# Decoding float64 weights by bits alone, in a three-layer kernel on one core

## The chip, the cores and the metric

One core of a Trainium2 chip runs the whole program. The metric is device time in microseconds (us) for one execution, from the first to the last instruction; the time of a kernel is the median of its runs. The engines are named as in the profile: PE is TensorE (PEld its weight loads), DVE is VectorE, ACT is ScalarE, POOL is GpSimd, SP is SyncE. The suffix q marks an engine's queue.

## The reference

Three layers follow one another on 4 sequences of 576 positions with 512 features.

1. Attention with 8 heads of 64, half of them masked to the last 32 positions (local), half to positions of the same residue modulo 32 (strided).
2. A mixture of 4 causal attention experts of which each position takes 2: projections wq, wk, wv, a gate, softmax, and wo.
3. A convolutional feed-forward layer:

```python
h = np.maximum(x @ w_in, 0.0)                      # w_in: 512 x 1024
conv_out = sum(conv_w[k] * hp[:, k:k + S, :] for k in range(3))   # hp: h padded by one position
gate = 1.0 / (1.0 + np.exp(-conv_out))
out = (h * gate @ w_out).astype(np.float32)        # w_out: 1024 x 512
```

The three weights of the last layer, w_in, conv_w and w_out, reach the chip as float64. Each value is two 32-bit words, the low word first; the high word holds the sign, the 11 bits of the exponent and the first 20 bits of the mantissa, the low word the other 32 bits.

## The kernel before, in words

The work is cut into generators, one for each tile or unit, and a hand-written list of letters says in which order the generators are started. S is the first layer (16 units: batch by local or strided by half of the heads), J loads and splits the projections of the second layer, P computes its projections, A its attention units, W prepares w_in and conv_w, O prepares w_out, M is a step of the third layer. A step of one generator ends at a `yield`, and all live generators are advanced in turn. The program is built with a model of the instructions' times that puts each engine's instructions in order, so work without a dependency can be placed ahead of its letter.

Products in higher precision are made from a high and a low part of each operand. For w_out, `split64` decodes a tile of 128 x 256 values and writes the high part (wout[0], rounded by an ACT copy) and the low part (wout[1]). For w_in, `w_wp` decodes 128 x 512 values into one float32 tile wi, and PE multiplies it with wo's transpose (tile wps, line 774): 2 halves of 4 tiles, so 8 tiles numbered 0 to 7 here. `w_taps` decodes conv_w into taps, 128 x 24.

The decode of one tile (`f64_parts`) has these steps:

- L719, ACT: the absolute value of the high word, into c (tile fc for w_in, oc for w_out, taps for conv_w);
- L720, DVE: c is held between two limits;
- L721, DVE: c shifted left by 3 and masked to 30 bits;
- L723, DVE: sign and top exponent bit of the high word ored with c, written over the high word. This is a float32 number a, cut after 20 bits of mantissa;
- L725, DVE: the mask keeps only the sign and exponent of a, into c;
- line 726, an ACT copy (it shows as L99): the low word is converted from integer to float and scaled;
- L727, POOL: the product of that and c, f.

Then L735 or L769 (on POOL and DVE in turn) or L789 (POOL) adds f: for w_in and the taps a + f is the value; for w_out the high part is copied from a, `sub` (L108) takes a minus the high part into c, and L735 adds f to that.

The staging tiles of w_in and conv_w (st, five buffers, shared with J) are filled by SP's queue; wi and fc have two buffers each. The tiles of w_out (ow, two buffers, shared with the output tile ob) are filled by POOL's queue, and oc shares two buffers with a tile of the third layer. The space of the staging pool is handed to wout once w_in and the taps are done (`rel`).

Of the kernel before, what the change touches and what calls it, by code (L numbers as in the profile page):

```python
# [7 lines left out]
F32 = mybir.dt.float32  # L8
# [5 lines left out]
ALU = mybir.AluOpType  # L14
# [34 lines left out]
def moe_stack_kernel(ctx, tc, qk_in, vloc, vstr, w_p, wo_t, w_in, conv_w, w_out, out):  # L49
# [27 lines left out]
    act, dve, gp = nc.scalar, nc.vector, nc.gpsimd  # L77
# [3 lines left out]
    def eng(kind, b=0):  # L81
        n = turn[kind] = turn.get(kind, -1) + 1
        s = ENG[kind].split("|")[0 if b < EARLY else -1]
        return s[n % len(s)]

    def e2(kind, b=0):
        return dve if eng(kind, b) == "V" else gp
# [10 lines left out]
    def copy_a(out, in_, scale=1.0):  # L98
        act.activation(out=out, in_=in_, func=ACTF.Copy, scale=scale)  # L99
# [7 lines left out]
    def sub(eng, out, a, b):  # L107
        eng.tensor_tensor(out=out, in0=a, in1=b, op=ALU.subtract)  # L108
# [77 lines left out]
    taps = wts.tile([128, 3 * KF], F32, name="taps")  # L186
# [523 lines left out]
    stg = tc.alloc_tile_pool(name="stg", bufs=2)  # L710
    woT = stg.tile([128, KD, E * D], F32, tag="woT", bufs=1, name="woT")

    def f64_parts(words, c):


        wl, wh = words[:, :, 0], words[:, :, 1]
        f = wl.bitcast(F32)
        cu = c.bitcast(U32)
        act.activation(out=c, in_=wh.bitcast(F32), func=ACTF.Abs)  # L719
        e2("w1").tensor_scalar(out=c, in0=c, scalar1=F64_LO, scalar2=F64_HI, op0=ALU.max, op1=ALU.min)  # L720
        dve.tensor_scalar(out=cu, in0=cu, scalar1=3, scalar2=0x3FFFFFFF,  # L721
                          op0=ALU.logical_shift_left, op1=ALU.bitwise_and)
        dve.scalar_tensor_tensor(out=wh, in0=wh, scalar=0xC0000000, in1=cu,  # L723
                                 op0=ALU.bitwise_and, op1=ALU.bitwise_or)
        dve.tensor_scalar(out=cu, in0=wh, scalar1=0xFF800000, scalar2=None, op0=ALU.bitwise_and)  # L725
        copy_a(f, wl, 2.0 ** -52)
        e2("wf").tensor_tensor(out=f, in0=f, in1=c, op=ALU.mult)  # L727
        return wh.bitcast(F32), f

    def split64(words, c, hi, lo):  # L730
        a, f = f64_parts(words, c)
        copy_a(hi, a)
        yield
        sub(e2("wc"), c, a, hi.bitcast(F32))
        e2("wa").tensor_tensor(out=lo, in0=c, in1=f, op=ALU.add)  # L735
        yield

    def w_proj(kk):
# [20 lines left out]
    def w_wp(hf, kk):  # L759
        cs = slice(512 * hf, 512 * hf + 512)  # L760
        t = stg.tile([128, 512, 2], U32, tag="st", bufs=ST_BUFS, name="st")
        nc.sync.dma_start(out=t.rearrange("p n w -> p (n w)"), in_=w_in[128 * kk:128 * kk + 128, cs].bitcast(U32))
        for _ in range(8):
            yield
        wi = stg.tile([128, 512], F32, tag="wi", name="wi")
        fc = stg.tile([128, 512], F32, tag="fc", name="fc")
        yield
        a, f = f64_parts(t, fc)
        e2("wa").tensor_tensor(out=wi, in0=a, in1=f, op=ALU.add)  # L769
        yield  # L770
        if kk == 0:
            wps[hf] = [ps_o.tile([128, 512], F32, tag=f"o{r}", name="wps") for r in range(2)]
        for r in range(2):
            nc.tensor.matmul(out=wps[hf][r], lhsT=woT[:, kk, 128 * r:128 * r + 128], rhs=wi,
                             start=kk == 0, stop=kk == KD - 1)
        if kk == KD - 1:
            yield
            for r in range(2):
                copy_a(wp[0][:, r, cs], wps[hf][r])
                sub(dve, wp[1][:, r, cs], wps[hf][r], wp[0][:, r, cs].bitcast(F32))  # L780
            if hf == 1:
                done.add("wp")

    def w_taps():
        t = stg.tile([128, 1024], U32, tag="st", bufs=ST_BUFS, name="ct")[:, 0:2 * 3 * KF].rearrange("p (n w) -> p n w", w=2)
        nc.sync.dma_start(out=t.rearrange("p n w -> p (n w)"), in_=conv_w.bitcast(U32))
        yield
        a, f = f64_parts(t, taps)
        gp.tensor_tensor(out=taps, in0=a, in1=f, op=ALU.add)  # L789
        yield  # L790
        done.add("taps")

    def w_out_part(f, hf):
        cs = slice(256 * hf, 256 * hf + 256)
        t = late["g"].tile([128, 256, 2], U32, tag="ob", bufs=2, name="ow")
        c = late["h"].tile([128, 256], F32, tag="t", name="oc")
        nc.gpsimd.dma_start(out=t.rearrange("p n w -> p (n w)"), in_=w_out[128 * f:128 * f + 128, cs].bitcast(U32))
        yield
        yield from split64(t, c, wout[0][:, f, cs], wout[1][:, f, cs])
        done.add(("wout", f, hf))  # L800
# [27 lines left out]
    def rel():  # L828
# [9 lines left out]
        "J": [w_proj(kk) for kk in range(KD)],  # L838
        "P": [u for b in range(B) for u in p_items(b)],
        "W": [w_init(), w_wo()] + [w_wp(hf, kk) for hf in range(2) for kk in range(KD)] + [w_taps()],  # L840
        "A": [u for b in range(B) for u in a_items(b)],
        "O": [w_out_part(f, hf) for f in range(KF) for hf in range(2)],
# [74 lines left out]
```

## Time and profile before

| | before |
|---|---|
| median of 3 runs | 471.08 us (469.86 to 472.1) |
| span of the profiled execution | 471.1 us |
| PE busy | 407.7 us (87%) |
| DVE busy | 349.1 us (74%) |
| ACT busy | 313.0 us (66%) |
| POOL busy | 187.6 us (40%) |
| mean granted TensorE clock | 0.946 of full speed |

The profiled execution's time is its span. Busy time is the sum of an engine's instructions; an engine that is busy for a small share of the whole may be full in one stage. "Idle before" is the time that an engine sat idle just ahead of an instruction, and the arrow names what ended it. A line can be that of a helper: L99 is `copy_a`, L108 is `sub`, so groups of such lines are told apart by their tiles.

### The profile page before, as it was taken

The numbers are of one execution on the slowest core, as the hardware profiler recorded it, in microseconds if no ns is written. First come the engines' busy times: TensorE is split into PE (matmuls) and PEld (weight loads), VectorE is DVE, ScalarE is ACT, GpSimd is POOL, SyncE is SP. The second block draws the span as 40 slices with busy tenths as digits, with TensorE's granted clock in tenths as the row PEclk, the third lists the DMA queues.
The fourth block names the chain that finished last, engine by engine and source line by source line (L and its number), as shares of the span: only waits on it lengthen the run. The fifth ranks groups of instructions, "written<-read, shape, count | busy, mean of one in ns | idle before, by whom it ended". The sixth has DMA issues, their size and how long they took to land.

```text
span 471.1 us, 12502 instructions
## 1 busy us (share of the span) xinstructions
PE 407.7 (87%) x4736; PEld 295.2 (63%) x4736; DVE 349.1 (74%) x941; ACT 313.0 (66%) x836; POOL 187.6 (40%) x253
## 2 busy tenths in 40 slices
PE   3367789966999898879999999998999989999994
PEld 2253456653567666647776767776777557787872
DVE  7399996777589998999777677669578676565550
ACT  3164642658777848777776688778499785667662
POOL 4356873443246565546533123214122324223231
PEclk9997898997689989978999999999999899999998
DMA  6995842433866664394333415424324273101011
GB/s 193 304 321 161 208 116 58 120 98 98 127 147 147 142 120 132 87 153 63 97 58 89 84 31 79 96 46 68 58 63 97 55 119 85 45 1 45 0 47 45
DMA packets 104956, 48.30 MB, mean 103 GB/s; under 512 B 77504, under 2 KB 100032, under 8 KB 104896
## 3 DMA queue, kind: packets, MB, share of 16 engines
q1 hardware_dynamic: 103616, 43.31, 41.3%
q0 software_dynamic: 1280, 4.20, 3.1%
q8 instruction: 37, 0.61, 0.6%
q14 instruction: 23, 0.19, 0.2%
HBM read 27.56 MB, written 4.72 MB: 69 GB/s over the span
## 4 chain that ended last, share of the span: by engine, by line
PE 47%; DVE 25%; DMA 10%; ACT 8%; issue 7%; SPq 1%; POOL 0%; POOLq 0%; ACTq 0%; DVEq 0%
PE o L111 6%; PE o L112 6%; PE o L113 5%; DMA apt<-pn 5%; PE zav L579 4%; PE hps L111 4%; PE asc L529 4%; DMA un<-in_dram 3%; PE hps L112 3%; PE hps L113 3%; DVE t L640 2%; DMA ow<-in_dram 2%; PE psq L111 2%; DVE apf L533 2%; PE psq L113 2%
## 5 line engine op out<-in xcount | busy, mean ns | idle before, releaser
L640 DVE SCALAR_TENSOR_TENSOR t<-hs,taps,t 128x256 f32<-128x256 f32 x144 | 80.7, 567 | 34.6 <-ACT t L99 33.4
L108 POOL TENSOR_TENSOR pn<-apf,pn 64x64 f16<-64x64 f32 (+4 forms) x40 | 33.9, 848 | 81.4 <-ACT pn L99 66.1
L108 POOL TENSOR_TENSOR gl<-t,gh 128x512 fp32r<-128x512 f32 x36 | 47.2, 1312 | 47.6 <-ACT gh L99 23.7
L112 PE MATMUL o<-wout,gl 128*128 128x512 f32 x144 | 59.0, 409 | 1.4 <-POOL gl L108 1.4
L111 PE MATMUL o<-wout,gh 128*128 128x512 f32 x144 | 54.8, 418 | 3.3 <-ACT gh L99 3.1
L113 PE MATMUL o<-wout,gh 128*128 128x512 f32 x144 | 56.5, 392 | 0.0
L539 ACT ACTIVATE apf<-apf,anm 64x64 f32<-64x64 f32 (+4 forms) x80 | 44.3, 554 | 10.6 <-DVE anm L533 10.5
L579 PE MATMUL zav<-apt,v 128*64 128x128 f16 (+2 forms) x720 | 37.1, 231 | 8.9 <-DMA apt<-pn 5.8
L533 DVE CUSTOM_DVE_ANT_0 apf<-asc,m_c 64x64 f32<-64x64 f32 (+4 forms) x80 | 32.5, 421 | 15.7 <-PE asc L529 15.2
L111 PE MATMUL psq<-xt,wqk 128*128 128x288 f16 x128 | 37.9, 296 | 6.9 <-DVE qk L478 4.2
L111 PE MATMUL hps<-z,wp 128*128 128x258 f32 x128 | 41.9, 327 | 0.5 <-ACT hs L103 0.5
L579 PEld LDWEIGHTS <-v 128*64 128x64 f16 (+1 forms) x720 | 25.4, 113 | 25.2 <-issue 12.6
L103 ACT ACTIVATE hs<-hps 128x257 f32<-128x257 f32 (+2 forms) x72 | 27.5, 381 | 20.2 <-PE hps L113 19.8
L99 ACT ACTIVATE t<-hs,taps 128x256 f32<-128x256 f32 x72 | 36.0, 505 | 3.8 <-DVE wout L735 1.1
L112 PE MATMUL psq<-xt,wqk 128*128 128x288 f16 x128 | 37.5, 293 | 0.0
L113 PE MATMUL psq<-xt,wqk 128*128 128x288 f16 x128 | 37.4, 292 | 0.0
L112 PE MATMUL hps<-z,wp 128*128 128x258 f32 x128 | 37.0, 289 | 0.0
L113 PE MATMUL hps<-z,wp 128*128 128x258 f32 x128 | 36.9, 288 | 0.0
L112 PEld LDWEIGHTS o<-wout,gl 128*128 128x128 f32 x144 | 27.0, 188 | 10.0 <-POOL gl L108 3.1
L111 PEld LDWEIGHTS o<-wout,gh 128*128 128x128 f32 x144 | 24.8, 190 | 11.8 <-ACT gh L99 5.7
L529 PE MATMUL asc<-qk,qk 64*128 64x288 f16 (+4 forms) x192 | 31.4, 288 | 0.0
L562 DVE SCALAR_TENSOR_TENSOR pn<-apf,aden,pn 64x64 f16<-64x64 f32 (+4 forms) x40 | 24.1, 604 | 9.5 <-ACT pn L99 9.3
(166 smaller groups left out, 1072.0 us busy)
## 6 DMA issues: line engine op xcount, KB each, us to landing
ow<-in_dram POOLq DMA_DIRECT2D x16, 256.0 KB, 3.9
st<-in_dram SPq DMA_DIRECT2D x8, 512.0 KB
out_dram<-ob SPq DMA_DIRECT2D x16, 256.0 KB
un<-in_dram SPq DMA_DIRECT2D x16, 252.0 KB
vs<-in_dram SPq DMA_DIRECT2D x32, 72.0 KB
vn<-in_dram SPq DMA_DIRECT2D x16, 128.0 KB
un<-in_dram SPq DMA_DIRECT2D x8, 240.0 KB
st<-in_dram SPq DMA_DIRECT2D x4, 386.0 KB
```

What stands on the lines that cost most here:

```text
L99: act.activation(out=out, in_=in_, func=ACTF.Copy, scale=scale)
L103: act.activation(out=out, in_=in_, func=ACTF.Relu)
L108: eng.tensor_tensor(out=out, in0=a, in1=b, op=ALU.subtract)
L111: nc.tensor.matmul(out=out, lhsT=ah, rhs=bh, start=first, stop=False)
L112: nc.tensor.matmul(out=out, lhsT=al, rhs=bh, start=False, stop=False)
L113: nc.tensor.matmul(out=out, lhsT=ah, rhs=bl, start=False, stop=last)
L529: nc.tensor.matmul(out=scs[par], lhsT=qk[a][p0:p0 + 64, 0, q0:q0 + rows], rhs=qk[l][p0:p0 + 64, 1, c0:c0 + cw], start=n == 0, stop=n == 2)
L533: dve.tensor_tensor_reduce(out=pfs[par][:, c0:c0 + cw], in0=scs[par], in1=m_c[:rows, S - w + c0 if rows == 128 else S - 128:][:, :cw], sca ...
L539: act.activation(out=pfs[par], in_=pfs[par], func=ACTF.Exp, scale=-1.0, bias=nm[:, par, len(cuts) - 1:len(cuts)], accum_out=den[:, par:par ...
L562: dve.scalar_tensor_tensor(out=pn[:, 1, :w], in0=pfs[par], scalar=den[:, par:par + 1], in1=pn[:, 0, :w], op0=ALU.mult, op1=ALU.subtract)
L579: nc.tensor.matmul(out=av[64 * par:64 * par + 64, 0:rows], lhsT=v2[a][:kk, kb, D * e:D * e + D], rhs=pts[par][:kk, l, kb], start=(kb == 0 ...
L640: dve.scalar_tensor_tensor(out=tv, in0=taps_at[i][n], scalar=w, in1=tv, op0=ALU.mult, op1=ALU.add)
```

## The change

The low word is no longer converted to a number. Its top three bits are shifted down by 29 and ored behind the 20 bits of mantissa from the high word, which gives all 23 bits of a float32. The function `f64_word` writes that value into c; mask, conversion, product and sum are gone. In `split64` the high part is copied from c, and `sub` writes c minus the high part straight into the low part. In `w_wp` the tile fc is gone, and wi is the tile that all steps of the decode write. The number of `yield` steps stays. The lower 29 bits of the low word are not used.

```diff
-    def f64_parts(words, c):
+    def f64_word(words, c):
         wl, wh = words[:, :, 0], words[:, :, 1]
-        f = wl.bitcast(F32)
         cu = c.bitcast(U32)
         act.activation(out=c, in_=wh.bitcast(F32), func=ACTF.Abs)
         e2("w1").tensor_scalar(out=c, in0=c, scalar1=F64_LO, scalar2=F64_HI, op0=ALU.max, op1=ALU.min)
         dve.tensor_scalar(out=cu, in0=cu, scalar1=3, scalar2=0x3FFFFFFF,
                           op0=ALU.logical_shift_left, op1=ALU.bitwise_and)
-        dve.scalar_tensor_tensor(out=wh, in0=wh, scalar=0xC0000000, in1=cu,
+        dve.scalar_tensor_tensor(out=cu, in0=wh, scalar=0xC0000000, in1=cu,
                                  op0=ALU.bitwise_and, op1=ALU.bitwise_or)
-        dve.tensor_scalar(out=cu, in0=wh, scalar1=0xFF800000, scalar2=None, op0=ALU.bitwise_and)
-        copy_a(f, wl, 2.0 ** -52)
-        e2("wf").tensor_tensor(out=f, in0=f, in1=c, op=ALU.mult)
-        return wh.bitcast(F32), f
+        dve.scalar_tensor_tensor(out=cu, in0=wl, scalar=29, in1=cu,
+                                 op0=ALU.logical_shift_right, op1=ALU.bitwise_or)

     def split64(words, c, hi, lo):
-        a, f = f64_parts(words, c)
-        copy_a(hi, a)
-        yield
-        sub(e2("wc"), c, a, hi.bitcast(F32))
-        e2("wa").tensor_tensor(out=lo, in0=c, in1=f, op=ALU.add)
+        f64_word(words, c)
+        copy_a(hi, c)
+        yield
+        sub(e2("wc"), lo, c, hi.bitcast(F32))
         yield
...
         wi = stg.tile([128, 512], F32, tag="wi", name="wi")
-        fc = stg.tile([128, 512], F32, tag="fc", name="fc")
-        yield
-        a, f = f64_parts(t, fc)
-        e2("wa").tensor_tensor(out=wi, in0=a, in1=f, op=ALU.add)
+        yield
+        f64_word(t, wi)
         yield
...
-        a, f = f64_parts(t, taps)
-        gp.tensor_tensor(out=taps, in0=a, in1=f, op=ALU.add)
+        f64_word(t, taps)
```

## Rows read from the trace of the kernel before

**Rows 1.** The page: PE's busy share in 40 slices, in tenths.
```profile
PE   3367789966999898879999999998999989999994
```
**Rows 2.** Busy time by stretch: length, PE, PEld, DVE, ACT, POOL (instructions), clock, DMA.
```profile
24.00:72.00 48.00, 35.14 (x661) 21.75 (x654) 47.47 (x82) 26.57 (x58) 33.22 (x33) 0.89 0.72 195
72.00:84.00 12.00, 12.00 (x166) 8.06 (x165) 7.25 (x20) 3.46 (x10) 3.83 (x5) 0.86 0.27 75
84.00:132.00 48.00, 39.10 (x442) 25.22 (x440) 32.59 (x121) 34.09 (x108) 18.42 (x30) 0.86 0.53 111
132.00:228.00 96.00, 84.93 (x1295) 63.03 (x1296) 90.08 (x243) 70.50 (x198) 54.27 (x66) 0.91 0.60 125
228.00:471.00 243.00, 228.31 (x1912) 171.36 (x1910) 157.41 (x445) 171.57 (x450) 68.64 (x96) 0.99 0.29 61
```
**Rows 3.** The chain that ended last: start, us, what.
```profile
89.32 3.00 DMA ow<-in_dram
...
98.91 3.95 DMA ow<-in_dram
```
**Rows 4.** DVE's groups by line, 24 to 72 us: count, busy us, mean ns, idle.
```profile
L723 DVE SCALAR_TENSOR_TENSOR st<-st,fc 128x512 uint32<-128x512 uint32 x8 | 7.5, 934 | 0.1
...
L725 DVE TENSOR_SCALAR fc<-st 128x512 uint32<-128x512 uint32 x8 | 3.5, 434 | 0.0
L769 DVE TENSOR_TENSOR wi<-st 128x512 f32<-128x512 f32 x3 | 2.7, 916 | 0.0
```
**Rows 5.** DVE's timeline in the same stretch: start us, us, instruction.
```profile
40.11 1.50 DVE L720 TENSOR_SCALAR fc<-fc 128x512 f32<-128x512 f32 x1
...
50.56 1.67 DVE L723 SCALAR_TENSOR_TENSOR st<-st,fc 128x512 uint32<-128x512 uint32 x1
...
57.28 0.68 DVE L723 SCALAR_TENSOR_TENSOR st<-st,fc 128x512 uint32<-128x512 uint32 x1
```
**Rows 6.** POOL's timeline in the same stretch.
```profile
40.05 1.29 POOL L727 TENSOR_TENSOR st<-st,fc 128x512 f32<-128x512 f32 x1 [1.50 <-issue]
...
50.20 1.48 POOL L727 TENSOR_TENSOR st<-st,fc 128x512 f32<-128x512 f32 x1
```
**Rows 7.** ACT's waits, 84 to 228 us: total, times, longest.
```profile
ACT oc L719 <- DMA ow<-in_dram: 5.7, 5, 2.6
```
**Rows 8.** DVE's groups by line, 132 to 228 us.
```profile
L108 DVE TENSOR_TENSOR oc<-ow,wout 128x256 f32<-128x256 f32 x10 | 6.2, 619 | 0.0
L720 DVE TENSOR_SCALAR oc<-oc 128x256 f32<-128x256 f32 x10 | 6.2, 616 | 1.2 <-ACT oc L719 1.0
...
L723 DVE SCALAR_TENSOR_TENSOR ow<-ow,oc 128x256 uint32<-128x256 uint32 x10 | 5.0, 502 | 0.1
...
L735 DVE TENSOR_TENSOR wout<-oc,ow 128x256 fp32r<-128x256 f32 x5 | 3.6, 725 | 0.0
```
**Rows 9.** Tile oc, the whole span: ns shortest/median/longest, first and last start.
```profile
L720 DVE TENSOR_SCALAR oc<-oc x16: 230/290/1349, 10.2 to 210.3; 128x256 f32<-128x256 f32 x16
...
L725 DVE TENSOR_SCALAR oc<-ow x16: 267/282/295, 11.7 to 212.0; 128x256 uint32<-128x256 uint32 x16
...
L108 DVE TENSOR_TENSOR oc<-ow,wout x16: 359/420/1474, 86.9 to 214.3; 128x256 f32<-128x256 f32 x16
```
**Rows 10.** POOL's groups by line, 132 to 228 us.
```profile
L727 POOL TENSOR_TENSOR ow<-ow,oc 128x256 f32<-128x256 f32 x10 | 9.1, 910 | 14.2 <-DVE z L108 5.0 <-DVE oc L725 4.5 <-ACT wout L99 2.0
```
**Rows 11.** Timelines of ACT (tiles 2 and 7) and PE (tiles 0, 5, 6 and 7).
```profile
35.74 0.65 ACT L719 ACTIVATE fc<-st 128x512 f32<-128x512 f32 x1
...
63.08 0.67 ACT L719 ACTIVATE fc<-st 128x512 f32<-128x512 f32 x1
...
37.56 3.73 PE L774 MATMUL wps<-wi,woT 128*128 128x512 f32 x4
...
67.14 1.88 PE L774 MATMUL wps<-wi,woT 128*128 128x512 f32 x4
...
80.98 3.70 PE L774 MATMUL wps<-wi,woT 128*128 128x512 f32 x8
```

## The prediction, made before the change was run

> **What bounds the kernel now.** I read the page first, then the busy time by stretch, then the chain of waits, then the groups by line and the timelines of single engines. The profiled execution has a span of 471.1 us, and the median of the runs shown is 471.08, so sums against the span are sums against the median.
>
> The slices show TensorE (PE) loosely filled at the start and at nine tenths or more later [rows 1]. Cut by stage, the picture is sharper [rows 2]. From 24 to 72 us VectorE (DVE) is busy 47.47 of 48 us while PE is busy 35.14: DVE is the bound. From 72 to 84 PE is full. From 84 to 132 nobody is full, which is a stretch of latencies. From 132 to 228 DVE is busy 90.08 of 96 and PE 84.93: both nearly full. After 228 PE is busy 228.31 of 243, so whatever arrives earlier at 228 ends earlier. Both kinds of decode work lie before that point: the eight tiles of w_in in 24 to 72, and the sixteen tiles of w_out, whose last mask starts at 212.0 [rows 9]. The chain of waits runs through DVE for most of the first stretch, and later holds two waits for a load of w_out, 3.00 and 3.95 us [rows 3].
>
> **The change, part by part.** Removed for each tile: the mask (L725, DVE), the conversion of the low word (a copy on ScalarE, ACT), the product (L727, GpSimd, here POOL) and, in all 25 places, the add or the add after the subtraction (L735, L769, L789). Added: one DVE instruction that shifts the low word and ors it in. The subtraction stays and now writes the low half itself. Tile fc goes, and the w_in decode builds its value in wi.
>
> *First stretch, 24 to 72, DVE's own instructions.* Removed: eight L725 at 434 ns, 3.5 us; three L769 that lie here, 2.7 us; the small L725 of the taps, 0.7 us (estimate: as long as the large ones or somewhat more); 6.9 us. Added: eight instructions of the form of L723, same tensors, same strided read. L723 takes 934 ns as a mean and 0.68 where nothing disturbs it [rows 4, 5]. I take 0.69, 5.5 us, and 0.7 for the taps: 6.2. Net −0.7; with the mean it is +1.3.
>
> The Trainium skill (Vector Engine (DVE) Microarchitecture Reference, section 5.2, Measured stream behaviour) speaks against this instruction: a stream whose elements are not pairs of adjacent words loses about 0.65 cycle per element, 1.73 ns per column with one such source. By it the added instruction would take about 0.96 us at 512 columns (an estimate), and eight of them 2.2 us more than I count. The trace disagrees: L723 reads every second word, writes every second word, and still took 0.68.
>
> *First stretch, waits of DVE behind POOL.* An L720 that started at 40.11, just after an L727 on POOL, took 1.50 and ended with it; an L723 at 50.56 took 1.67 under the L727 of 50.20, against 0.68 at 57.28 [rows 5, 6]. I count seven DVE instructions here that stretched by 0.5 to 1.1 us under an L727 or L769 and that stay in the kernel: 6.2 us beyond the shortest of their kind. All of these POOL instructions go. Two of eight L723 were hit, one of them under an instruction that goes, so the added eight should be hit about once: +1.0. About 1 us of waiting will fall onto other POOL instructions that move up. So −6.2 + 2.0 − 0.7 = **−5 us**. Ends: −7 if all of it is returned, +1.3 if nothing is and the added instructions take the mean. It passes on whole, for DVE has no idle time here and PE 13 us of it.
>
> *84 to 228: the load of w_out.* ACT sat 5.7 us, five times, before its first decode instruction, waiting for the load [rows 7]; everything behind it in ACT's order waited too. The tile (two buffers) is now free after the added instruction; before, it was held through mask, product, copy, subtraction and add. The next load can be issued that much sooner. Two such waits lie on the chain, 6.95 us [rows 3]. I take **−2 us**: the load is started sooner by some microseconds, but its issue stands in POOL's order, and the next decode still needs one of two value tiles. Ends 0 and −6.
>
> *132 to 228, DVE.* Removed ten L725 at 0.28 and five L735 at 725 ns: 2.8 + 3.6 = 6.4. Added ten of L723's form at 502 ns: 5.0. Net −1.4. Of waits behind POOL, ten L720 average 616 ns against a median of 290, ten L108 of oc 619 against 420: 5.3 us [rows 8, 9]. L727 is 9.1 of POOL's 54.27 us here, and with the five L735 on POOL, put at L727's 910 ns, about a quarter [rows 2, 10]: I take 1.3 of the 5.3. Sum −2.7. DVE is 94% and PE 88% full, so neither alone sets the pace: about half passes, **−1.5 us**; ends +1 and −6.
>
> *At nothing:* the conversions taken from ACT, 25 in all, sixteen in a range where ACT is busy 70.50 of 96 and 34.09 of 48 [rows 2]; without that cover they would be worth up to their own 12 us (an estimate: eight at the 0.65 that L719 takes on the same tile [rows 11], sixteen on half the columns at two thirds of it).
>
> Sum: 471.1 − 5 − 2 − 1.5 = **462.6**, so 462.5.
>
> **Rivals.**
>
> *The wait for wi (slower).* Before, ACT's first decode instruction of tile k needed fc, free after the product of tile k−2. Now it writes wi, free only after PE has multiplied tile k−2. Tile 2's started at 35.74, while the multiplication of tile 0 ran from 37.56 to 41.29: 5.6 us later. Tile 7's started at 63.08, and the multiplication of tile 5 ended at 69.02: 5.9 us later. For the six tiles it is 2.8 to 7.1 us [rows 11]. Queued behind on ACT are the copies of scores and of attention rows of the first layer, and DVE waits for those. For it: DVE's work would then no longer fill the stretch. Against: the multiplications of tiles 6 and 7 ran only from 80.98, when PE got to them, so the w_in chain has slack; and the decode itself is shorter by mask, product and add. It decides where the delays of three tiles in a row reach the first layer: three times 2.8 to 4 us, some +8 in place of −5, with the other terms as they are: 475.
>
> *Nothing moves.* PE is full in 72 to 84 and 94% after 228; if PE work is already in order behind other things, DVE's time returned becomes idle time. Then about 470.
>
> *More comes through.* All ends at once, −7, −6, −6, on the same instructions: 452. For it: the same waits behind POOL return twice, and ACT's 12 us on top.
>
> **How the numbers follow.** Half a per cent, 2.4 us, is about what a measurement of this kernel tells from no change. Forecast (454 to 468.7): 0.62. More comes through: 0.08. Nothing moves: 0.17. The wait for wi: 0.13. Faster 0.70, same 0.17, slower 0.13. The instructions are put in order at build time from a model of their times, so a shorter decode rearranges neighbours; I allow ±4 us around the forecast for it. Leaving out the outermost cases on either side, the range is 454 to 472.
>
> **What would show it.** Right: DVE in 24 to 72 no longer full or the stretch shorter by some 5 us; the first w_out low half written before 84; the L720 group nearer its shortest; ACT's wait for the w_out load nearly gone; the added instruction at 0.65 to 0.7 and 0.42 us. Wrong: ACT waiting for PE ahead of L719 in the first stretch, long PE waits for wi, or the added instruction near 1 us. A forecast of −8.5 us fails most simply if the first layer is paced by loads (its input tiles, rather than DVE) once DVE has room.

## The result, and the profile after

The changed kernel takes **476.99 us** (median of 12 runs, 473.18 to 481.23), the kernel before 470.9 (12 runs, 469.17 to 473.93): a ratio of 1.0102 with a 95% interval of 1.0071 to 1.0134. It is 1% slower. I had forecast 462.5, with a range of 454 to 472. Medians are over all runs; ratios leave out the runs that are over 1.5% above the fastest of their kernel.

Where a run lists both, its time is 1.7 us above its span: the profiled execution of the changed kernel has a span of 471.5 and a time of 473.18, the lowest of its twelve. So this profile shows the best of its runs, 0.4 us above the span of 471.1 before; it can explain why nothing was gained, and not all of the loss. (By the same 1.7 us the profiled execution of before stands at about 472.8, not at the median as I had put it.) In the changed kernel the decode has the lines L718 (absolute value), L719 (limits), L720 (shift), L722 (sign and top exponent bit) and L724 (the added instruction).

The page of the changed kernel, PE's busy share in 40 slices of 11.8 us:

```profile
PE   3458599979899679997997999999899989999994
```

Against [rows 1], the sixth slice is 9 for 8 and the ninth and tenth are 7 and 9 for 6 and 6: PE is fed sooner. Slices 14 and 15 (153 to 177 us) are 6 and 7 for 8 and 9, slices 19 and 22 are 7 for 9, and only 16 to 18 are higher, 9 for 8, 8 and 7: most of what was won is lost there.

Busy time by stretch, in the columns of [rows 2]:

```profile
24.00:72.00 48.00, 36.32 (x628) 23.34 (x627) 39.98 (x83) 23.33 (x54) 17.89 (x20) 0.89 0.79 213
72.00:84.00 12.00, 12.00 (x218) 8.27 (x219) 10.13 (x33) 5.65 (x14) 3.22 (x5) 1.00 0.40 102
84.00:132.00 48.00, 43.01 (x444) 26.81 (x440) 34.41 (x113) 34.18 (x105) 14.48 (x21) 0.79 0.51 108
132.00:228.00 96.00, 84.49 (x1234) 61.90 (x1234) 82.81 (x226) 67.65 (x180) 38.90 (x48) 0.93 0.51 111
228.00:471.00 243.00, 226.94 (x1940) 170.49 (x1939) 152.59 (x446) 170.30 (x448) 66.55 (x95) 0.99 0.32 63
```

DVE has 39.98 us of work in the first stretch for 47.47, and 82.81 in 132 to 228 for 90.08. These two windows do not hold the same work as before: the last of the eight w_in tiles has slipped behind 72 us, and over 24 to 84 us DVE has 4.6 us less (50.11 for 54.72). Over the whole execution each engine but PE does less, and the end does not come sooner. PE is busy 412.1 us for 407.7 with the same 4736 matmuls; from 84 to 132 us 444 of them take 43.01 us at a mean granted clock of 0.79, where 442 took 39.10 at 0.86.

DVE's groups by line in 24 to 72 us, in the columns of [rows 4]:

```profile
L722 DVE SCALAR_TENSOR_TENSOR wi<-st,wi 128x512 uint32<-128x512 uint32 x7 | 5.0, 710 | 0.1
L724 DVE SCALAR_TENSOR_TENSOR wi<-st,wi 128x512 uint32<-128x512 uint32 x7 | 4.9, 706 | 0.0
L719 DVE TENSOR_SCALAR wi<-wi 128x512 f32<-128x512 f32 x7 | 3.9, 561 | 0.2 <-ACT wi L718 0.2
```

Tiles st and oc over the whole span, in the columns of [rows 9]:

```profile
L724 DVE SCALAR_TENSOR_TENSOR wi<-st,wi x8: 674/680/1118, 34.7 to 75.0; 128x512 uint32<-128x512 uint32 x8
...
L724 DVE SCALAR_TENSOR_TENSOR oc<-ow,oc x16: 403/416/1405, 11.7 to 182.1; 128x256 uint32<-128x256 uint32 x16
...
L108 DVE TENSOR_TENSOR wout<-oc,wout x16: 376/416/1052, 86.9 to 184.0; 128x256 fp32r<-128x256 f32 x16
```

ACT's waits, the first from 24 to 84 us, the second from 84 to 228, as in [rows 7]:

```profile
ACT wi L718 <- PE wps L768: 1.9, 2, 1.3
...
ACT oc L718 <- DMA ow<-in_dram: 1.9, 2, 1.2
```

The added instruction has medians of 680 and 416 ns. The sign instruction fell from 934 to 710 ns as a mean [rows 4], and ACT's wait for the w_out load from 5.7 us to 1.9 [rows 7]. The last L108 of w_out starts at 184.0 instead of 214.3 [rows 9]: w_out is ready 30 us sooner. The wait for wi, my slower rival, is 1.9 us of idle ACT in all. It shows more in when the last w_in tile, tile 7, starts on ACT:

```profile
72.42 0.68 ACT L718 ACTIVATE wi<-st 128x512 f32<-128x512 f32 x1 [1.27 <-PE wps L768]
```

It started at 63.08 before [rows 11], and now starts when PE has released wi. So w_in's product comes no sooner: the last subtraction on it (DVE, L108, tile wp) starts at 86.26 us, where it started at 86.32.

Now the places where the lead is lost. Tiles as before, on PE and DVE: the second layer's q and k projections (psq), the third layer's first product (hps), the maxima of the first layer's strided units of the third of the four batches (nms, 124 to 180 us) and that batch's v projection (psv, 170 to 270 us, twenty of L111). The kernel before:

```profile
L111 PE MATMUL psq<-xt,wqk x128: 282/286/463, 84.5 to 364.3; 128*128 128x288 f16 x128
...
L111 PE MATMUL hps<-z,wp x128: 278/286/561, 128.8 to 437.8; 128*128 128x258 f32 x128
...
L225 DVE TENSOR_REDUCE nms<-pp x2: 436/444/453, 145.6 to 164.0; 128x16 f32<-128x288 f32 x2
...
L111 PE MATMUL psv<-wvg,xt x20: 273/274/298, 219.4 to 255.8; 128*128 128x260 f16 x16, 128*64 128x260 f16 x4
```

The changed kernel:

```profile
L111 PE MATMUL psq<-xt,wqk x128: 283/286/448, 77.1 to 366.6; 128*128 128x288 f16 x128
...
L111 PE MATMUL hps<-z,wp x128: 278/287/584, 121.3 to 438.3; 128*128 128x258 f32 x128
...
L225 DVE TENSOR_REDUCE nms<-pp x2: 436/444/452, 160.9 to 175.6; 128x16 f32<-128x288 f32 x2
...
L111 PE MATMUL psv<-wvg,xt x20: 273/274/286, 234.1 to 259.4; 128*128 128x260 f16 x16, 128*64 128x260 f16 x4
```

The first psq leads by 7.4 us and the first hps by 7.5. From 24 to 132 us PE did 1290 matmuls for 1269, and from 132 to 228 it did 1234 for 1295. The maxima of the same batch's local units (tile nm) ran at 128.7 and 141.6 us and now run at 121.1 and 145.4: between these two the lead turns into a lag. The maxima of its strided units, at 145.6 and 164.0 before, now run at 160.9 and 175.6, and the projection that needs this batch's rows starts at 234.1 instead of 219.4.

What took their place shows in busy time of 128 to 162 us: all instructions; then DVE, ACT (and POOL) on tile oc, the decode of w_out; then on tile t, the third layer's taps and gate. The kernel before:

```profile
128.00:162.00 34.00, 32.66 (x610) 25.01 (x609) 30.68 (x82) 25.73 (x67) 18.34 (x21) 0.95 0.73 147
...
128.00:162.00 34.00, 7.43 (x15) 1.29 (x3) 3.24 (x4) 0.95 0.73 147
...
128.00:162.00 34.00, 5.56 (x10) 3.82 (x7) 1.29 (x1) 0.95 0.73 147
```

The changed kernel:

```profile
128.00:162.00 34.00, 30.43 (x390) 22.03 (x390) 31.56 (x82) 24.74 (x62) 15.28 (x22) 0.90 0.46 122
...
128.00:162.00 34.00, 13.00 (x30) 5.11 (x12) 0.90 0.46 122
...
128.00:162.00 34.00, 10.34 (x14) 6.05 (x11) 2.62 (x2) 0.90 0.46 122
```

DVE is as full as before, with the same 82 instructions. But w_out and the third layer take 13.00 + 10.34 of its 31.56 us, where they took 7.43 + 5.56 of 30.68. For the rest, nearly all of it the first two layers, 8.2 us are left instead of 17.7. PE gets 390 matmuls done in place of 610, for the many small ones of the first layer were put off. I read this as the faster decode running ahead of work that the end was waiting for; the experiments bear that out in part.

### The profile page after: what moved, and what is told of

It reads as the page before. It is cut to its first block, busy times and chain, and to the rows that moved or that the text cites. A ratio compares the mean times of both kernels' runs of the same rounds, so it can differ in the third digit from the quotient of the medians.

```text
span 471.5 us, 12407 instructions
## 1 busy us (share of the span) xinstructions
PE 412.1 (87%) x4736; PEld 297.0 (63%) x4736; DVE 333.9 (71%) x929; ACT 307.1 (65%) x811; POOL 150.5 (32%) x215
## 4 chain that ended last, share of the span: by engine, by line
PE 42%; DMA 4%; ACT 3%; DVE 3%; issue 2%; POOLq 0%; POOL 0%; SPq 0%; ACTq 0%; DVEq 0%
PE o L111 6%; PE o L112 6%; PE o L113 5%; DMA apt<-pn 4%; PE zav L579 4%; PE asc L529 4%; PE hps L111 4%; PE hps L113 3%; PE hps L112 3%; PE psq L111 2%; PE psq L113 2%; PE psq L112 2%; DVE t L640 1%; PE psv L111 1%; DVE apf L533 1%
## 5 line engine op out<-in xcount | busy, mean ns | idle before, releaser
L640 DVE SCALAR_TENSOR_TENSOR t<-hs,taps,t 128x256 f32<-128x256 f32 x144 | 82.9, 579 | 35.3 <-ACT t L99 34.3
L108 POOL TENSOR_TENSOR gl<-t,gh 128x512 fp32r<-128x512 f32 x36 | 47.8, 1328 | 48.6 <-ACT gh L99 27.0
L108 POOL TENSOR_TENSOR pn<-apf,pn 64x64 f16<-64x64 f32 (+4 forms) x40 | 34.0, 852 | 88.4 <-ACT pn L99 65.0
L111 PE MATMUL o<-wout,gh 128*128 128x512 f32 x144 | 55.1, 419 | 1.0 <-ACT gh L99 0.9
L111 PE MATMUL hps<-z,wp 128*128 128x258 f32 x128 | 42.0, 328 | 4.5 <-ACT z L99 3.3
L533 DVE CUSTOM_DVE_ANT_0 apf<-asc,m_c 64x64 f32<-64x64 f32 (+4 forms) x80 | 32.9, 424 | 17.0 <-PE asc L529 14.8
L111 PE MATMUL psq<-xt,wqk 128*128 128x288 f16 x128 | 37.5, 293 | 1.5 <-DVE qk L478 0.7
L111 PEld LDWEIGHTS hps<-z,wp 128*128 128x128 f32 x128 | 24.4, 191 | 13.1 <-ACT hs L103 4.3
L94 POOL COPY bd<-lp 32x640 f32<-32x640 f32 (+1 forms) x32 | 20.6, 644 | 33.3 <-PE avs L385 12.0
```

The lines of the kernel that those rows point to most:

```text
L94: (dve if e == "V" else gp).tensor_copy(out=out, in_=in_)
L111: nc.tensor.matmul(out=out, lhsT=ah, rhs=bh, start=first, stop=False)
L533: dve.tensor_tensor_reduce(out=pfs[par][:, c0:c0 + cw], in0=scs[par], in1=m_c[:rows, S - w + c0 if rows == 128 else S - 128:][:, :cw], sca ...
L640: dve.scalar_tensor_tensor(out=tv, in0=taps_at[i][n], scalar=w, in1=tv, op0=ALU.mult, op1=ALU.add)
```

## The experiments

Each was timed in five rounds beside the kernel before on the same chip; the medians of before in these five groups are 470.6, 470.7, 470.8, 471.8 and 471.6 us. Edits are to the changed kernel where nothing else is said. A table at the end of this section holds DVE's times from 128 to 162 us for all of them.

### One half of the change alone, and the tile fc

The changed kernel once more, with no edit, for a second profile:

> The changed kernel once more, for a second profile. Three theories of why it is slower. Order: the instructions returned to VectorE change the order that the build gives to PE; third-layer steps come early, the second layer of batch 2 late, and PE starves between 240 and 262 us. Clock: most runs lose their time in stretches at the lower granted clock, which the first profile (the fastest of its runs) hardly shows. Wait for wi: the decode of w_in waits for PE. All expect about 477 us here. By order the second profile starves at the same place, and lead and lag at the same points differ by under 1 us; by clock a run of 476 us or more shows a stretch before 230 us with a granted clock lower by 0.1 or more than in the first profile and loses there what it is longer.

477.13 us, 1.0142 [1.0088, 1.0197]. The second profile (span 473.0) shows the same crowding: 13.31 and 10.14 us for w_out and the third layer in 128 to 162, of 31.88. PE is busy 18.94 of 22 us from 240 to 262, for 18.29 in the first profile and 20.20 in the kernel before, as the order foretold; its first-layer maxima come 1.3 and 1.4 us before those of the first profile, a little more than the 1 us foretold. The profiled run took 474.7 us, so the test of the clock, which asked for a run of 476 or more, was not made.

The new decode for w_in and the taps alone; `f64_parts` is back for w_out:

```diff
     def split64(words, c, hi, lo):
-        f64_word(words, c)
-        copy_a(hi, c)
+        a, f = f64_parts(words, c)
+        copy_a(hi, a)
         yield
-        sub(e2("wc"), lo, c, hi.bitcast(F32))
+        sub(e2("wc"), c, a, hi.bitcast(F32))
+        e2("wa").tensor_tensor(out=lo, in0=c, in1=f, op=ALU.add)
```

> New decode for w_in and the taps, old decode for w_out. Wait for wi: the whole loss is here, 475 us or more. Order: the first 84 us end 3 to 5 us earlier as in the changed kernel, the w_out tiles come at their old pace, third-layer steps are not early, so 466 to 470. Clock: undecided.

463.37 us, 0.9842 [0.9796, 0.9887], better than either theory said. The other half alone, new for w_out and old for w_in and the taps:

```diff
+        fc = stg.tile([128, 512], F32, tag="fc", name="fc")
         yield
-        f64_word(t, wi)
+        a, f = f64_parts(t, fc)
+        e2("wa").tensor_tensor(out=wi, in0=a, in1=f, op=ALU.add)
```

> Old decode for w_in and the taps, new decode for w_out. Wait for wi: no loss, 467 to 471. Order: wout is ready early, third-layer steps run early, and PE starves later: 473 to 479.

472.33 us, 1.0013 [0.9972, 1.0054], between the two ranges. The halves alone give −7.2 us (463.37 − 470.58) and nothing; together they give +6. The effects do not add, so the loss is not the price of any one instruction.

The decode of w_in works in fc as before and only its last instruction writes wi, so ACT never waits for PE to release wi:

```diff
-        dve.scalar_tensor_tensor(out=cu, in0=wl, scalar=29, in1=cu,
+        dve.scalar_tensor_tensor(out=cu if to is None else to.bitcast(U32), in0=wl, scalar=29, in1=cu,
...
+        fc = stg.tile([128, 512], F32, tag="fc", name="fc")
         yield
-        f64_word(t, wi)
+        f64_word(t, fc, wi)
```

> The changed kernel, but the w_in decode works in fc as before and only the last instruction writes wi. Wait for wi: back to 470 or less. Order and clock: 474 to 479, unless the order happens to change.

469.53 us, 0.9991 [0.9959, 1.0024]: 7 us better than the changed kernel, as if the wait for wi were the cause. The same edit on the half that gains tells whether it is:

> The kernel with the new decode for w_in and the taps alone, w_out as before, and the w_in decode working in fc. Wait for wi: faster than the same without fc, 460 or less. Crowding: no wait to take away, 461 to 466. Scatter: up to 5 us either way.

462.9 us, 0.9814 [0.9784, 0.9844], beside 0.9842 [0.9796, 0.9887] without the edit. Where the decode of w_in is all that is new, the wait for wi costs nothing that can be measured. Two kernels below say the same: with nine w_out tiles later ACT waits 4.9 us for wi and the time is 463.06, and the slowest kernel of all, 480.84, keeps fc and has no such wait. So the wait is not the cause of a 14 us miss; what fc gives in the full change I put down to the order.

### The order of the work

The first-layer units of the third batch ahead of the rest, in the changed kernel and, as a control, in the kernel before:

```diff
-    order += mix("A" * 6, "O" * 4) + mix("A" * 4, "O" * 12, "M" * 4, "P" * 9, "SSSS")
+    order += mix("A" * 6, "O" * 4) + list("SSSS") + mix("A" * 4, "O" * 12, "M" * 4, "P" * 9)
```

> The changed kernel with the four first-layer units of batch 2 started ahead of the twelve w_out tiles and four third-layer steps they were mixed with. Crowding (the decode of w_out and early third-layer steps push the first layer of batch 2 back on VectorE from 128 to 162 us, and PE starves from 240 to 262): the maximum of its second strided unit comes before 165 us instead of 175.6, the last first-layer scores on PE before 242 instead of 247.8, time 470 or less. Wait for wi: no effect on the loss, 475 to 479. Scatter (any new order moves the time by several us, whatever the work): anything between 465 and 480, and not in step with the first layer.

> The same early start in the kernel before, as a control. Crowding: little to win, since w_out comes slowly there: 468 to 472. Scatter: a move of 4 us or more either way.

466.78 us, 0.9916 [0.9882, 0.995], and 477.03 us, 1.01 [1.0056, 1.0144]: one order, opposite effects. In the changed kernel the marks of the crowding were met (second maximum at 139.1 us, last scores at 237.7). The control came out as the scatter had it, 6 us slower and outside the 468 to 472 of the crowding, though its own maxima came sooner too, at 130.4 and 144.6.

Six of the twelve w_out tiles later, again in both kernels; then three and nine of them later in the changed one:

```diff
-    order += mix("A" * 6, "O" * 4) + mix("A" * 4, "O" * 12, "M" * 4, "P" * 9, "SSSS")
+    order += mix("A" * 6, "O" * 4) + mix("A" * 4, "O" * 6, "M" * 4, "P" * 9, "SSSS")
...
-        order += mix("A" * 5, "P" * 4, "M" * MM[b][0], sn)
+        order += mix("A" * 5, "P" * 4, "O" * (6 if b == 1 else 0), "M" * MM[b][0], sn)
```

> The changed kernel with six of the sixteen w_out tiles started later, beside the attention of batch 1. Crowding: VectorE has less decode from 132 to 180, the first layer of batch 2 comes earlier, 466 to 472. Wait for wi: 475 to 479. Scatter: anything between 465 and 480.

> The kernel before with six w_out tiles started later. The same two cases: 468 to 473, or 464 or less (the changed kernel in the same order took 463.7).

> Three w_out tiles started later instead of six (which gave 463.7). Crowding: between, 466 to 474. Scatter: anything from 463 to 480. In every case the span should be 225 us, within 3, more than the time of the last first-layer scores on PE, as in the ten profiles so far.

> Nine w_out tiles started later. Crowding: like six or slightly better, 461 to 466, until the third layer waits for w_out. Scatter: anything from 463 to 480. Span again 225 us, within 3, behind the last first-layer scores.

463.74 us, 0.9842 [0.9812, 0.9872]; the kernel before with it 476.76, 1.0056 [1.0017, 1.0095]; with three later 463.11, 0.9819 [0.9764, 0.9874]; with nine 463.06, 0.9871 [0.9824, 0.9918]. Six and three later came out below the ranges of the crowding, nine inside it, and the control in neither of its two cases. The span lies 227.1 and 223.4 us behind the last first-layer scores with three and nine later, as expected, but 232.7 with the next edit: so it is no rule.

The four third-layer steps out of that stretch, again in both, then together with the six later tiles:

```diff
-    order += mix("A" * 6, "O" * 4) + mix("A" * 4, "O" * 12, "M" * 4, "P" * 9, "SSSS")
+    order += mix("A" * 6, "O" * 4) + mix("A" * 4, "O" * 12, "P" * 9, "SSSS")
...
-    order += ["M"] * (36 - 4 - sum(map(sum, MM)))
+    order += ["M"] * (36 - sum(map(sum, MM)))
```

> The changed kernel with the first four third-layer steps started later, beside the attention of batch 1; the w_out tiles keep their places. If it is the early third-layer steps that push the first layer back, their elementwise work leaves VectorE before 162 us, the last first-layer scores come before 242 us, and the time is 470 or less. If it is the decode of w_out itself, the last scores stay at 245 or later and the time at 473 or more.

> The kernel before with the first four third-layer steps started later. If the order helps because w_out now comes early, little changes here: 468 to 473. If it helps whatever the decode, 464 or less, and the decode's own worth is what the changed kernel in the same order (462.1) is below it.

> The changed kernel with both moves: third-layer steps later and six w_out tiles later. 459 to 464; if the third layer then waits for w_out or PE lacks work that it had, 465 or more.

462.1 us, 0.9825 [0.978, 0.9869]; the kernel before with it 473.35, 1.0028 [0.9998, 1.0059]; both edits 464.92, 0.9823 [0.9773, 0.9874], so they do not add either. The last scores come at 230.7 us in the first of these, as the case of the early third-layer steps had it.

The subtraction of w_out moved from DVE to POOL, in the table that gives each kind of operation its engine:

```diff
-'wc': 'V'
+'wc': 'P'
```

> The changed kernel with the sixteen subtractions that give w_out's low parts on GpSimd, as the last addition of every second tile was before: 16 times about 0.42 us less on VectorE. Crowding: the tiles come somewhat slower and VectorE has more room, 466 to 474. Scatter: anything from 463 to 480.

465.83 us, 0.9882 [0.9843, 0.992]. Four kinds of edit (the third batch ahead, w_out later, the third layer later, the subtraction on POOL), which take work off DVE's stretch or let the first layer go ahead in it, each bring the changed kernel from 477 to between 462 and 467.

Two more edits speak against that as the whole story. The later third-layer steps with fc kept:

> The changed kernel with third-layer steps later, and the w_in decode working in fc. If the wait of the w_in decode for PE costs anything, below 460; if not, 460 to 465 as without fc.

480.84 us, 1.0152 [1.0101, 1.0203]. By the crowding it should have been among the fast ones. And the first-layer units of the fourth batch ahead, first alone, then with the six later tiles:

```diff
-        order += mix("A" * 5, "P" * 4, "M" * MM[b][0], sn)
-        order += mix("A" * 5, "P" * (9 if b < B - 1 else 0), "M" * MM[b][1], sn)
+        order += list(sn) + mix("A" * 5, "P" * 4, "M" * MM[b][0])
+        order += list(sn) + mix("A" * 5, "P" * (9 if b < B - 1 else 0), "M" * MM[b][1])
```

> The changed kernel with the first-layer units of batch 3 at the front of the two stretches they are mixed into; w_out, the third layer and batch 2 keep their places. If the end follows the first layer, the last first-layer scores come 5 us earlier or more (242 or less) and the time is 470 or less. If the loss sits elsewhere, the scores may come earlier and the time stays at 474 or more.

> The same on top of six w_out tiles later (463.7 alone, last scores at 234.0). If the end follows the first layer, last scores before 231 and 462 or less; once PE no longer starves, nothing more is to be won by it: 462 to 466.

470.36 us, 0.9986 [0.9952, 1.0019], and 461.37 us, 0.9747 [0.9706, 0.9789], the fastest kernel of this study. In the first of the two the last first-layer scores (tile scs on PE) start at 237.2 instead of 247.8 us in the changed kernel's profile, and its span is 471.2 for 471.5: the end does not follow from the first layer's last unit.

DVE in 128 to 162 us in the profile of each kernel: its busy time, what of it is on tile oc and on tile t, and the difference, which is left for the rest, nearly all of it the first two layers.

| kernel | median us | busy | oc | t | left |
|---|---|---|---|---|---|
| changed, first profile | 477.0 | 31.56 | 13.00 | 10.34 | 8.2 |
| changed, second profile | 477.1 | 31.88 | 13.31 | 10.14 | 8.4 |
| fourth batch ahead | 470.4 | 30.18 | 12.72 | 9.94 | 7.5 |
| fc kept | 469.5 | 30.94 | 10.71 | 5.21 | 15.0 |
| third batch ahead | 466.8 | 33.50 | 13.89 | 4.77 | 14.8 |
| subtraction on POOL | 465.8 | 29.89 | 8.75 | 5.15 | 16.0 |
| both later | 464.9 | 30.75 | 11.55 | 6.50 | 12.7 |
| six tiles later | 463.7 | 31.09 | 11.65 | 7.47 | 12.0 |
| w_in and taps alone | 463.4 | 31.82 | 9.68 | 6.75 | 15.4 |
| third layer later | 462.1 | 31.51 | 8.97 | 8.19 | 14.4 |
| six tiles later, fourth batch ahead | 461.4 | 29.62 | 11.05 | 7.46 | 11.1 |
| third layer later, fc kept | 480.8 | 31.46 | 6.17 | 9.80 | 15.5 |
| three tiles later | 463.1 | 31.13 | 9.98 | 6.56 | 14.6 |
| nine tiles later | 463.1 | 33.22 | 10.56 | 7.33 | 15.3 |
| w_in and taps alone, fc kept | 462.9 | 32.07 | 9.92 | 5.96 | 16.2 |
| w_out alone | 472.3 | 24.77 | 8.60 | 5.19 | 11.0 |
| before | 470.9 | 30.68 | 7.43 | 5.56 | 17.7 |
| before, third batch ahead | 477.0 | 29.22 | 8.23 | 5.90 | 15.1 |
| before, six tiles later | 476.8 | 27.62 | 8.45 | 7.65 | 11.5 |
| before, third layer later | 473.4 | 25.91 | 11.51 | 0.00 | 14.4 |

With the new decode of w_in, 7.5 to 8.4 us left go with times of 470 to 477, and 11 to 16 left with 461 to 470, but for the slowest of all (third layer later, fc kept). With the old decode of w_in the times are 471 to 477 whatever is left, from 11 to 18: 11.0 with w_out alone takes 472.3, and 11.1 with six tiles later and the fourth batch ahead takes 461.4. So what is left does not order the times by itself. The stretches 84 to 132 and 128 to 162 us, first the kernel with the third layer later:

```profile
84.00:132.00 48.00, 39.69 (x465) 24.71 (x464) 41.61 (x144) 35.48 (x111) 15.18 (x25) 0.79 0.60 127
128.00:162.00 34.00, 29.56 (x559) 22.09 (x559) 31.51 (x83) 26.72 (x66) 15.65 (x20) 0.95 0.86 159
```

The same with fc kept as well:

```profile
84.00:132.00 48.00, 34.33 (x379) 22.04 (x376) 38.74 (x151) 31.67 (x103) 14.48 (x26) 0.82 0.52 125
128.00:162.00 34.00, 31.49 (x485) 22.92 (x484) 31.46 (x76) 26.46 (x67) 14.83 (x18) 0.87 0.72 137
```

The tiles nms and psv as above, again first the kernel with the third layer later:

```profile
L225 DVE TENSOR_REDUCE nms<-pp x2: 443/445/447, 144.3 to 167.0; 128x16 f32<-128x288 f32 x2
...
L111 PE MATMUL psv<-wvg,xt x20: 271/274/285, 221.5 to 251.2; 128*128 128x260 f16 x16, 128*64 128x260 f16 x4
```

And with fc kept as well:

```profile
L225 DVE TENSOR_REDUCE nms<-pp x2: 432/438/443, 151.9 to 171.4; 128x16 f32<-128x288 f32 x2
...
L111 PE MATMUL psv<-wvg,xt x20: 273/279/442, 232.8 to 264.0; 128*128 128x260 f16 x16, 128*64 128x260 f16 x4
```

The first is back near the times of the kernel before (145.6 and 219.4), and ends these twenty ahead of it (251.2 for 255.8). The second is late at the projection by as much as the changed kernel, though DVE had 15.5 us for the first layers: there is a second way to be late. The lines above say where it begins: from 84 to 132 us, ahead of the crowded stretch, its PE does 379 matmuls, where 465 are done with the third layer later alone. Why the order leaves PE less to do there these runs do not show.

## Why the prediction was wrong

**The savings came, and more than I counted.** Over the whole execution, where no work slips across a border, DVE's decode of w_in and the taps (tiles fc, wi and taps in the steps of the decode) fell from 29.2 to 20.9 us, by 8.3 where I counted 5, and that of w_out (tile oc) from 39.8 to 32.5, by 7.3 where I counted 2.7 for ten of its sixteen tiles. The added instruction, put at 0.69 us, has a median of 0.68. The Trainium skill (Vector Engine (DVE) Microarchitecture Reference, section 5.2, Measured stream behaviour on trn2) gives 1.73 ns a column for a source that hops 4 KiB at every element. I carried that over to a step of two words, which its table does not hold, and my estimate of 0.96 us from it is not borne out here. ACT's wait for the w_out load went nearly away. The limits of w_in's decode are nearer their shortest, 561 ns as a mean for 887 before.

Of the marks of being right one failed: the first low half of w_out is written at 86.9, not before 84. Of the signs of being wrong two showed in part. ACT does wait for PE ahead of its first decode instruction. PE's wait for the first layer's input (tile un) rose from 2.9 to 6.6 us in 24 to 84, though the first psq came earlier all the same.

**The failed step** is the passage from these terms to the end: "It passes on whole, for DVE has no idle time here", and for rearranged neighbours "I allow ±4 us around the forecast". The reason in the first is that DVE had no idle time; with the change DVE is idle 8.0 of the 48 us from 24 to 72, for 0.5 before, and PE is busy there 36.32 us for 35.14. Part of the gain did pass on, as far as the first psq and hps, 7.4 and 7.5 us early. It was then given back while the instructions behind came in another order: in 128 to 162 us DVE runs thirty instructions on tile oc where it ran fifteen, and the first layer's maxima follow 11.6 to 15.3 us later. My sum took the stretch from 84 to 228 as the same work with shorter pieces. The runs show moves of the order alone worth up to 16 us (477.0 against 461.4), several times what I had allowed. The miss of 14.5 us is of that size, but the runs do not show that this crowding is all of it.

The same comparison, made in one order for both decodes, gives what the change is worth when the order is not against it. The ratio of the two ratios is 0.982 with the third batch ahead (0.9916 / 1.01), 0.979 with six tiles later, 0.980 with the third layer later, each within about half a per cent (the two half intervals, squared and added): 8.5 to 10 us, beside my sum of 8.5. In the written order it is 1.0102. This fits the terms and does not prove them: I chose these orders to relieve the changed kernel, and all three made the kernel before slower or left it (1.0028 to 1.01), so part of each ratio may be that loss. And with fc kept, the last of these orders gives 1.012 in place of 0.980 (1.0152 / 1.0028). The best orders known of each take 470.9 and 461.4, with four orders tried of the kernel before and nine of the changed one.

**The rivals.** "The wait for wi" named a time near the one measured, 475, but for a wrong reason: the wait is there and holds the last w_in tile 9.3 us back, but taking it away changed nothing that can be measured in the half that gains. "Nothing moves" is nearer to what happened: in the first stretch DVE's returned time did become idle time, and behind it other work. I had no rival in which the time returned lets w_out and the third layer run ahead and hold up the first layer, though the hand-written list starts both in one `mix`.

**What is shown and what is open.** Shown: the first hps still comes early and the first layer of the third batch late, the loss comes from the two halves together, it goes away under four kinds of edit of the order or the engine, and none of the three tried on the kernel before helps it. Argued, and only in part borne out: that the crowding of DVE at 128 to 162 is the mechanism. The rival that the expectations call scatter, that any new order moves the time by several us whatever the work, is not excluded: nine orders of the changed kernel span 461.4 to 477.0 us, four of the kernel before 470.9 to 477.0, and the written order may simply be a bad one for the new decode. The kernel with fc kept and the third layer later, 480.8, and the one with the fourth batch ahead, 470.4 with the crowding in place, are against it as the whole story. Why a tile of its own for the decode is worth −7 us in one order and +19 in another (480.8 against 462.1) was not settled. Nor was the rest of the 6 us, that which the profile of the fastest run does not hold: the runs of the changed kernel above 477 us have mean granted clocks of 0.928 to 0.942, those below 474.1 of 0.948 to 0.958, and beside one another on one chip its median clock is 0.941 (six runs) for 0.951 of the kernel before (23 runs). If all of PE's 412 us went with that, it would be about 4 us, an estimate. Whether the clock is cause or consequence no run here tells apart.

## What to carry to other kernels

Where a build puts instructions in order from a hand-written list and a model of times, a saving in one stage is a change of the order in all later ones: price it by its instructions, and then ask which later work the faster producer pulls ahead and whose place that takes on the fuller engine. Judge such a change in two or three orders, each run with the old and the new code, before it is called good or bad. If two halves of a change do not add up, look at the order before looking for a costly instruction.

## What the runs showed of the hardware that I had not expected

DVE still waits behind POOL though the products are gone. DVE's timeline in the changed kernel:

```profile
45.40 1.36 DVE L720 TENSOR_SCALAR wi<-wi 128x512 uint32<-128x512 uint32 x1
...
48.97 0.38 DVE L720 TENSOR_SCALAR wi<-wi 128x512 uint32<-128x512 uint32 x1
```

POOL's beside it:

```profile
45.16 1.31 POOL L108 TENSOR_TENSOR sp<-sp,nm 128x640 f32<-128x640 f32 x1
```

The same instruction takes 1.36 us when it starts under a POOL subtraction, and ends 0.29 us after it (46.76 against 46.47), and 0.38 us when it starts with POOL idle. In the kernel before it was alike: the limits that started at 40.11 ended at 41.61, 0.27 us after the product on POOL (41.34) and not with it [rows 5, 6].

The added form, with every second word of its first operand read, took 0.68 us for 512 columns and 0.416 for 256, so each further column cost 1.03 ns. Its medians are within 0.02 us of those of the sign instruction beside it (0.69 and 0.416), and at 256 columns the same as that of the subtraction L108, which reads and writes every word.
